# The last two heads of a linear attention: a sixteenth product per block, or spare rows of the attention output filled by way of DRAM

## The chip, the cores and the metric

The kernel runs on one core of a Trainium2 chip. Its time is what the device needs for one execution, in microseconds (us); the median of three runs before the change is 650.78 us, the lowest 650.26 and the highest 651.06. A core has TensorE (PE in the profile; PEld are its weight loads), VectorE (DVE), ScalarE (ACT), GpSimd (POOL) and SyncE (SP), which here only issues DMAs. "DMA" are the sixteen transfer engines that they share.

## The reference

The input `x` is 1 x 2048 x 640, layer-normalised, and goes into two branches. One is a linear attention of 32 heads of 20 with a feature map of two softmaxes; the other is a gelu MLP with 1536 hidden units. The result is `x + attention * silu(MLP)`.

```
q, k, v = (xn @ wqkv) split into 32 heads of 20
phi_q = concat[softmax(q w_phi), softmax(-q w_phi)]      (40 features a head; phi_k alike)
num = phi_q @ (phi_k^T v);  den = phi_q . sum_s phi_k + 1e-6
s = (num / den, heads side by side: 640 columns) @ wo
out = x + s * silu(gelu(xn @ w1 + b1) @ w2 + b2)
```

## The kernel before, in words

Most of the program (up to about 535 us of the profiled execution's span) makes queries, keys and values and runs eleven of the twelve units of the MLP. This study is about what comes behind: the twelfth unit's second matrix, the numerators of the attention, and the output projection. There the 2048 tokens are worked on in four chunks of 512, in `ORDER = (2, 3, 0, 1)`, and everything lies transposed: rows are features, columns are tokens.

The normalised query features lie in DRAM in one tensor per chunk, `phi_t[c]`, with 1280 rows (32 heads x 40). The four token tiles of each chunk write it (L1069, `phi_t<-eq`, from `q_norm`), and `load_phi` (L1086) reads it back: five loads of 240 rows (`phT<-phi_t`, 480 KB each, L1091, groups j = 0 to 4, three heads for each of two halves) and one of the last two heads' 80 rows (160 KB, L1093, j = 5).

`num` (L1097) makes the numerators. For j = 0 to 4 two products with the block-diagonal state `bdk` fill rows 0 to 63 and 64 to 127 of a PSUM bank. A half holds three heads, so 60 rows of it carry data and four are zero. ACT copies the bank to `oT` in the rounded form (L1106), and DVE writes what the rounding left as a second plane (L1107). Group j = 5, the last two heads, takes two products with `bdl` (L1110) and one more pair of evictions (L1112, L1113), into `oTl`, which holds its 40 rows three times in different roundings.

`finish` (L1145) makes a block of 128 output rows: for each j three products with `wo_s[j]` (high by high, high by low, low by high: `PASSES`), and a sixteenth, `wol` by `oTl`, which covers the three passes of the last two heads at once. Behind it DVE multiplies by the gate, POOL adds the residual (L1158, L1159), and SP stores the block. Five blocks (d = 0 to 4) make a chunk, and the numerators of the next chunk stand behind block 3 of each chunk.

Two more things matter. `make_wol` (L1077) makes `wol` from a loaded `raw` (L1074) with two DVE operations, a cast (`wolh`) and one that writes `wol`; before, both stand in the MLP's last `down` (L990). `down` works in the order d = 0 to 2 together, then 3, then 4, and its `mid` steps put other work between its products; the first chunk's `num` is one.

The order is written by hand: the program runs under a manual schedule, so that each engine does its instructions in the order in which the code issues them. All loads and stores of this part are issued by SP, in one order. SP's DMAs count on eight semaphores in turn, and each waits until the one eight places ahead of it has landed; a DMA that waits for an engine's result holds up every DMA behind it.

Of the kernel before, what the change touches and what calls it, by code (L numbers as in the profile page):

```python
# [15 lines left out]
P = 128  # L16
NT = S // P
NCH = 4
# [28 lines left out]
def hedgehog_gated_mlp_kernel(ctx: ExitStack, tc: tile.TileContext, x, xt_in, wqk, bd, wv, wo, w1, b1, w2, b2, out_t):  # L47
# [33 lines left out]
    def slab(dt, name, shape=(P, 2, D)):  # L81
        return slabs.tile(list(shape), dt, tag="S", name=name)
# [18 lines left out]
    wq_dram = dram.tile([2, P, 2, HALF], F32, name="wq_dram")  # L101
    z_dram = dram.tile([1440], F32, name="z_dram")
    st_dram = dram.tile([NT // 2, 2, P, 2], F32, name="st_dram")

    nc.gpsimd.memset(hmask, 1.0)
    nc.gpsimd.affine_select(out=hmask, in_=hmask, pattern=[[-DH, 6]], compare_op=OP.is_ge, fill=0.0, base=0,
# [872 lines left out]
    def act_lo(ps, hs):  # L979
        nc.vector.tensor_tensor(hs[:, 1], ps, hs[:, 0].bitcast(F32), op=OP.subtract)  # L980
        return hs
# [89 lines left out]
    def wol_raw():  # L1071
        raw = row([P, D], F32, "raw")
        for r in range(3):
            nc.sync.dma_start(raw[40 * r:40 * r + 40, :], wo[640:680, :])  # L1074
        return raw

    def make_wol(raw):  # L1077
# [4 lines left out]
                                       op0=OP.mult, op1=OP.add)  # L1082
        return wol


    def load_phi(c, js, home=None):  # L1086
        out = {}
        for j in js:
            ph = slab(F32, "phT", (P, 2, CW)) if home is None else home.tile([P, 2, CW], F32, tag="L", name="phT")
            if j < 5:  # L1090
                nc.sync.dma_start(ph[:120], phi_t[c][240 * j:240 * j + 240, :].rearrange("(e p) t -> p e t", p=120))  # L1091
            else:
                nc.sync.dma_start(ph[:80, 0], phi_t[c][1200:, :])  # L1093
            out[j] = ph
        return out

    def num(phi, oT, js):  # L1097
        for j in js:
            ph = phi.pop(j)
            po = bankB()  # L1100
            if j < 5:
                for e in range(2):
                    nc.tensor.matmul(po[64 * e:64 * e + 64, :], bdk[:120, 2 * j + e, :], ph[:120, e, :],  # L1103
                                     start=True, stop=True)
                o2 = oT[0][j]
                nc.scalar.activation(o2[:, 0], po[:], AF.Copy)  # L1106
                nc.vector.tensor_tensor(o2[:, 1], po[:], o2[:, 0].bitcast(F32), op=OP.subtract)  # L1107
            else:
                for a, b in ((0, 64), (64, 120)):
                    nc.tensor.matmul(po[a:b, :], bdl[:80, a:b], ph[:80, 0], start=True, stop=True)  # L1110
                o2 = oT[1]
                nc.scalar.activation(o2[:120, 0], po[:120], AF.Copy)  # L1112
                nc.vector.scalar_tensor_tensor(o2[:120, 1], o2[:120, 0].bitcast(F32), lowsel[:120, :],  # L1113
                                               po[:120], op0=OP.mult, op1=OP.add)

    JA, JB = (0, 1, 2), (3, 4, 5)

    def new_oT(home):
        return ([home.tile([P, 2, 512], F32R, tag="S" if home is slabs else "L", name="oT") for _ in range(5)],
                slab(F32R, "oTl", (P, 2, 512)))  # L1120

    xres, gates, wols = {}, {}, []
    ORDER = (2, 3, 0, 1)

    def load_res(i):
# [10 lines left out]
    def gate(i):  # L1136
        if i < NCH * KC:
            c, d = divmod(i, KC)
            c = ORDER[c]
            if c < 2:  # L1140
                y = ys[d][:, c, :]
                nc.scalar.activation(y, y, AF.Silu, bias=b2t[:, d:d + 1])
                gates[c, d] = y

    def finish(c, d, oT, last):  # L1145
        steps = [(wo_s[j][:, b, d * P:(d + 1) * P], oT[0][j][:, a, :]) for j in range(5) for a, b in PASSES]
        steps.append((wols[0][:120, d * P:(d + 1) * P], oT[1][:120, 1, :]))
        xr, gt = xres.pop((c, d)), gates.pop((c, d))
        end = last and d == KC - 1
        parts = (slice(0, W2), slice(W2, 512))  # L1150
        for k, sl in enumerate(parts):
            if end or k == 0:
                mv = sl if end else slice(0, 512)
                ps = bankB()
                for n, (w, o) in enumerate(steps):
                    nc.tensor.matmul(ps[:, mv], w, o[:, mv], start=n == 0, stop=n == 15, skip_group_check=True)  # L1156
            g = gt[:, sl]
            nc.vector.tensor_tensor(g, ps[:, sl], g, op=OP.mult)  # L1158
            (nc.vector if last else nc.gpsimd).tensor_tensor(xr[:, sl], g, xr[:, sl], op=OP.add)  # L1159
            if last:  # L1160
                nc.sync.dma_start(out_t[d * P:(d + 1) * P, c * CW + sl.start:c * CW + sl.stop], xr[:, sl])
        if not last:
            nc.sync.dma_start(out_t[d * P:(d + 1) * P, c * CW:(c + 1) * CW], xr[:])
# [20 lines left out]
    for unit in range(units):  # L1184
# [71 lines left out]
        if not more:  # L1256
            xstack.close()
            ctx.enter_context(tc.tile_pool(name="pad", bufs=1)).tile([P, 16], F32, name="lpad")
            late = ctx.enter_context(tc.tile_pool(name="late", bufs=13, reuse_waits="tile"))
# [4 lines left out]
        if not more:  # L1264
            wolr = wol_raw()
        turn(qdone)
        qdone = qs
        for t in QN.get(unit + 1, ()):
            qe[t] = q_load(t)
        next(w1f, None)  # L1270
        dn = down(g, w2g, hs, 0)
        next(dn)
        h12 = act_lo(*h12)
        next(q1, None)
        next(w1f, None)
# [47 lines left out]
    phin.update(load_phi(ORDER[1], JB))  # L1323
    gate(0)
    gate(1)

# [14 lines left out]

    lq = late_q((7,))
    for ci, c in enumerate(ORDER):
        if ci + 1 < NCH:
            oTn = new_oT(late if ci % 2 else slabs)
        for d in range(KC):
            load_res(ci * KC + d + 4)
            finish(c, d, oT, ci == NCH - 1 and d >= 3)
            next(lq, None)
            gate(ci * KC + d + 2)  # L1350
            if ci == 0 and d < 2:
                next(lq, None)
            if ci + 2 < NCH and d == 1:
                phi = load_phi(ORDER[ci + 2], JA, late if ci % 2 else None)
            if ci + 1 < NCH and d == 3:
                num(phin, oTn, range(6))
            if ci + 2 < NCH and d == 3:
                phin = {**phi, **load_phi(ORDER[ci + 2], JB)}
        if ci + 1 < NCH:
            oT = oTn  # L1360
    ffn.close()
# [2 lines left out]
def _layout(A_x, A_wqkv, A_w_phi, A_wo, B_w1, B_b1, B_w2, B_b2):  # L1364
    import numpy as np
    a = {k: np.asarray(v) for k, v in dict(x=A_x, wqkv=A_wqkv, wphi=A_w_phi, wo=A_wo, w1=B_w1, b1=B_b1,
                                           w2=B_w2, b2=B_b2).items()}
    wqk = np.zeros((2, KC, P, FOLD_W), a["wqkv"].dtype)
    bd = np.zeros((P, 6, DH), a["wphi"].dtype)
    wo = np.zeros((680, D), a["wo"].dtype)  # L1370
    for k in range(10):
        wo[64 * k:64 * k + 60] = a["wo"][60 * k:60 * k + 60]
    wo[640:] = a["wo"][600:]
# [38 lines left out]
```

## Time and profile before

| what | value |
|---|---|
| time, median of 3 runs (lowest, highest) | 650.78 us (650.26, 651.06) |
| span of the profiled execution, first to last instruction | 649.0 us |
| PE busy | 643.7 us (99%) |
| DVE, ACT, POOL busy | 485.1, 238.1, 408.9 us |
| DMA, mean of the span | 210 GB/s |

The profiled execution's own time is not listed apart from its span; the median of the runs lies 1.78 us above the span, and that difference is the work around the first and the last instruction. In the profile's timelines a row gives a start, a length, the engine, the line and the tiles, and the number of instructions; brackets give the idle time ahead of it on that engine and what ended it. Rows whose engine ends in q (SPq) are instructions of the engine's queue, such as the issue of a DMA. A full-precision product (L1103, L1110) appears as two matrix passes, so `x20` there are ten products.

### The profile page before, as it was taken

Reading aid. Unit: us, or ns where it says so; the run is one execution under the profiler, and the core shown is the slowest. Engines: PE = TensorE matmul, PEld = TensorE weight load, DVE = VectorE, ACT = ScalarE, POOL = GpSimd, SP = SyncE. Lnnn points to the kernel's source line nnn. Section 1 sums busy time; section 2 is a strip of 40 time slices with the busy share of each in tenths; the row PEclk is TensorE's granted clock in tenths of the full one; section 3 lists DMA queues with packets and bytes.
Section 4 is the critical chain, followed back from the end, with each engine's and each line's share of the span. In section 5 each row is a group of like instructions: output and inputs, shape, how many; then the busy total and the mean of one; then the engine's idle time right before and its main releaser. Section 6 shows DMA issues by size and latency. Waiting matters only on the chain.

```text
span 649.0 us, 11412 instructions
## 1 busy us (share of the span) xinstructions
PE 643.7 (99%) x4379; PEld 559.1 (86%) x4379; DVE 485.1 (75%) x736; ACT 238.1 (37%) x345; POOL 408.9 (63%) x375
## 2 busy tenths in 40 slices
PE   9999999999999999999999999999999999999997
PEld 9999999999999998888888888888888886766866
DVE  5887976789867787587988877768889899853132
ACT  3622423425243447244243346641231524032130
POOL 2876477897987756857878865355463966342321
PEclk9999999999999999999999999999999999999999
DMA  9477286494312477365986998794969499999952
GB/s 346 113 238 228 57 303 197 107 309 147 123 42 74 152 263 262 103 217 170 317 236 236 254 409 285 144 350 163 183 238 243 67 267 198 304 242 248 291 207 81
DMA packets 167119, 136.53 MB, mean 210 GB/s; under 512 B 89890, under 2 KB 131106, under 8 KB 166682
## 3 DMA queue, kind: packets, MB, share of 16 engines
q1 hardware_dynamic: 164330, 124.22, 65.9%
q10 hardware_dynamic: 2736, 11.60, 4.8%
q8 instruction: 34, 0.56, 0.4%
q14 instruction: 19, 0.16, 0.1%
HBM read 87.41 MB, written 48.38 MB: 209 GB/s over the span
## 4 chain that ended last, share of the span: by engine, by line
PE 96%; DMA 1%; DVE 1%; SPq 0%; issue 0%; DVEq 0%
PE pB L998 24%; PE pA L411 23%; PE pB L969 23%; PE pB L1156 11%; PE pA L724 6%; PE pB L1103 2%; PE pA L174 2%; PE kv L491 2%; PE qV L724 1%; DMA folds<-in_wqk_dram 1%; PE qY L724 1%; DVE y L1007 1%; PE pB L1110 1%; DMA phi_t<-eq 0%; PE pA L397 0%; DVE wolh L1080 0%
## 5 line engine op out<-in xcount | busy, mean ns | idle before, releaser
L998 PE MATMUL pB<-hs,w2s 128*128 128x512 f32 x720 | 165.7, 389 | 0.0
L998 PEld LDWEIGHTS pB<-hs,w2s 128*128 128x128 f32 x720 | 135.0, 188 | 28.8 <-DVE y L1007 0.8
L969 PE MATMUL pB<-xp,w1s 128*128 128x512 f32 x324 | 81.3, 389 | 0.0
L969 PE MATMUL pB<-xd,w1s 128*128 128x512 f32 x324 | 79.3, 389 | 0.0
L452 POOL TENSOR_TENSOR eq<-eq,rc 128x1280 f32<-128x1280 f32 x16 | 37.9, 2368 | 55.3 <-DVE rc L1060 38.1
L1156 PE MATMUL pB<-oT,wo 128*128 128x512 f32 (+1 forms) x315 | 72.3, 381 | 0.0
L969 PEld LDWEIGHTS pB<-xd,w1s 128*128 128x128 f32 x324 | 60.8, 188 | 12.6
L969 PEld LDWEIGHTS pB<-xp,w1s 128*128 128x128 f32 x324 | 60.8, 188 | 12.6
L1156 PEld LDWEIGHTS pB<-oT,wo 128*128 128x128 f32 x315 | 57.2, 188 | 13.8 <-PE pB L1103 2.5
L1007 DVE TENSOR_TENSOR y<-pB,y 128x512 f32<-128x512 f32 x100 | 63.1, 676 | 1.4 <-PE pB L998 1.4
L974 ACT ACTIVATE pB<-pB,b1t 128x512 f32<-128x512 f32 x48 | 31.8, 662 | 78.8 <-DVE pB L1237 28.9
L411 PE MATMUL pA<-wk,xp 128*128 128x320 f32 x384 | 59.6, 310 | 0.0
L439 ACT ACTIVATE e<-e 128x1280 f32<-128x1280 f32 x32 | 40.6, 1272 | 50.0 <-POOL e L430 50.0
L411 PEld LDWEIGHTS pA<-wk,xp 128*128 128x128 f32 x384 | 56.9, 188 | 0.1
L430 POOL TENSOR_TENSOR e<-nr,e 128x640 f32<-128x640 f32 x32 | 46.0, 1437 | 16.4 <-DVE nr L429 16.3
L452 POOL TENSOR_TENSOR e<-e,rc 128x1280 f32<-128x1280 f32 x16 | 37.8, 2369 | 20.2 <-DVE rc L479 20.2
L1047 POOL TENSOR_TENSOR ez<-eq,zrep 128x1280 f32<-128x1280 f32 x16 | 47.3, 2959 | 2.0 <-DMA eq<-e_dram 2.0
L519 POOL TENSOR_TENSOR w1s<-raw,w1s 128x640 fp32r<-128x640 f32 (+1 forms) x18 | 26.2, 1458 | 27.6 <-ACT w1s L518 27.6
L411 PE MATMUL pA<-wv,xp 128*128 128x320 f32 x240 | 37.0, 310 | 0.0
L1159 POOL TENSOR_TENSOR xres<-gt,xres 128x256 f32<-128x256 f32 x20 | 14.3, 735 | 35.3 <-DVE gt L1158 24.9
L149 POOL TENSOR_TENSOR w2s<-raw,w2s 128x640 fp32r<-128x640 f32 x23 | 36.1, 1592 | 0.2 <-ACT w2s L147 0.2
L411 PEld LDWEIGHTS pA<-wv,xp 128*128 128x128 f32 x240 | 35.5, 188 | 0.1
(190 smaller groups left out, 1140.4 us busy)
## 6 DMA issues: line engine op xcount, KB each, us to landing
raw<-in_w_dram SPq DMA_DIRECT2D x42, 320.0 KB, 6.7
e_dram<-e ACTq DMA_DIRECT2D x16, 640.0 KB, 3.9
eq<-e_dram SPq DMA_DIRECT2D x16, 640.0 KB
phi_t<-eq SPq DMA_DIRECT2D x64, 160.0 KB, 4.3
phT<-phi_t SPq DMA_DIRECT2D x20, 480.0 KB, 10.1
xt<-in_x_dram SPq DMA_DIRECT2D x16, 320.0 KB, 6.1
xres<-in_xt_dram SPq DMA_DIRECT2D x20, 256.0 KB, 9.1
out_dram<-xres SPq DMA_DIRECT2D x18, 256.0 KB, 5.1
```

The lines of the kernel that those rows point to most:

```text
L149: eng.tensor_tensor(sl[:, 1, :], raw, sl[:, 0, :].bitcast(F32), op=OP.subtract)
L411: nc.tensor.matmul(ps[:, hf, :HALF], stat_x(q, o, k, a), ws[k][:, b, hf * HALF:(hf + 1) * HALF], start=n == 0, stop=n == 3 * KC - 1)
L430: rest = lambda: nc.gpsimd.tensor_tensor(e5[:, :, :, 1, :], nr[:, :, :, None].to_broadcast([P, 2, 16, DH]), e5[:, :, :, 0, :], op=OP.subtract)
L439: nc.scalar.activation(ef, ef, AF.Exp)
L452: nc.gpsimd.tensor_tensor(e3, e3, rc[:, :, None].to_broadcast([P, 64, DH]), op=OP.mult)
L724: nc.tensor.matmul(bank[ch], q_x(blk, a, q), p_weight(base, f, w, k)[:, b], start=ch not in seen and n == 0, stop=n == len(mms) - 1, skip_ ...
L969: nc.tensor.matmul(bank[ch][:], tl[:, a, off + wo_:off + wo_ + P], mov(blk, b), start=new and n == 0, stop=n == len(mms) - 1, skip_group_c ...
L974: nc.scalar.activation(ps, ps, AF.Gelu_apprx_tanh, bias=b1t[:, f:f + 1])
L998: nc.tensor.matmul(ps[:], ws[i][:, b, d * P:(d + 1) * P], hs[o][i][:, a, :], start=i == n == 0, stop=(i, n) == (GF - 1, 2), skip_group_che ...
L1007: nc.vector.tensor_tensor(y, ps[:], y, op=OP.add)
L1047: nc.gpsimd.tensor_tensor(zv, ef, zf, op=OP.mult)
L1156: nc.tensor.matmul(ps[:, mv], w, o[:, mv], start=n == 0, stop=n == 15, skip_group_check=True)
```

## The change

Three of the four chunks (2, 3 and 0) lose the sixteenth product. Their last two heads' 40 rows go into the four spare rows of each half of `oT` (rows 60 to 63 and 124 to 127, five groups: 2 x 4 x 5 = 40 rows), and the host lays the matching rows of `wo` at those places. Chunk 1, the last one, keeps the product.

The 40 rows change partition on the way, and go through DRAM: `load_rest` loads the last two heads' features (`phR`) early, `num_rest` makes the rows (chunks 2 and 3 together in one bank, chunk 0 in another), evicts both planes to `oR` and stores them in `r_dram` (512 KB and 256 KB), and `put_rest` brings them into `oT` with two DMAs per chunk, each of four rows of 20 KB (`4x5120`). As rows 60 to 63 of a half are now written by a DMA, the evictions of these chunks go in two parts of 60 rows each. `oT` is one tile for all five groups, with two buffers. `make_wol` and its loads move behind the middle of the tail, the first `num` moves one step ahead in `down`, and `num` comes ahead of the gate in the loop.

```diff
+    def load_rest(*cs):
+        ph = slab(F32, "phR", (P, 2, CW))
+        for e, c in enumerate(cs):
+            nc.sync.dma_start(ph[:80, e], phi_t[c][1200:, :])
+        return ph, len(cs)
+    def num_rest(ph, n):
+        po, o2 = bankB(), slab(F32R, "oR", (P, 2, CW))
+        at = slice(0, 64 * n)
+        for e in range(n):
+            nc.tensor.matmul(po[64 * e:64 * e + 64, :], bdl[:80, :64], ph[:80, e, :], start=True, stop=True)
+        split_o(po, o2, at)
+        rest = r_dram[next(rests)]
+        nc.sync.dma_start(rest[at], o2[at].bitcast(F32).rearrange("p s t -> p (s t)"))
+        return rest
+    def split_o(po, o2, *parts):
+        for at in parts:
+            nc.scalar.activation(o2[at, 0], po[at], AF.Copy)
+        for at in parts:
+            nc.vector.tensor_tensor(o2[at, 1], po[at], o2[at, 0].bitcast(F32), op=OP.subtract)
+    def num(phi, oT, parts=(slice(0, 60), slice(64, 124))):
+        for j in range(KC):
...
+            split_o(po, oT[:, j], *parts)
+    def put_rest(oT, oR, r):
+        for e in range(2):
+            nc.sync.dma_start(oT[64 * e + 60:64 * e + 64].bitcast(F32).rearrange("p j s t -> p j (s t)"),
+                              oR[r + 20 * e:r + 20 * e + 20].rearrange("(i j) t -> i j t", j=KC))
-        steps.append((wols[0][:120, d * P:(d + 1) * P], oT[1][:120, 1, :]))
+        if c == ORDER[-1]:
+            steps.append((wol[:120, d * P:(d + 1) * P], oTl[:120, 1, :]))
...
-            phi = load_phi(ORDER[0], range(6))
+            phi = load_phi(ORDER[0], range(KC))
+            phr = load_rest(*ORDER[:2]), load_rest(ORDER[2])
...
         next(dn)
+        if not more:
+            rest.append(num_rest(*phr[0]))
...
         if not more:
+            rest.append(num_rest(*phr[1]))
             break
...
-    oT = new_oT(late)
-    phin = load_phi(ORDER[1], JA, late)
+    oT, oTn = oTs
+    put_rest(oT, rest[0], 0)
+    phin = load_phi(ORDER[1], JA)
...
     def first_num():
-        wols.append(make_wol(wolr))
-        yield
         yield
         yield
-        num(phi, oT, range(6))
+        num(phi, oT)
         yield
...
+            if ci == 1 and d == 4:
+                wolr = wol_raw()
+            if ci == 2 and d == 2:
+                wol = make_wol(wolr)
```

Where the instructions stand now is told by their order on each engine. On PE, from the last `down` on (`hs` by `w2s`) to the first blocks of the projection, before:

```order
L998 MATMUL pB<-hs,w2s 128x512 x48
L1103 MATMUL pB<-phT,bdk 64x512 x10
L1110 MATMUL pB<-phT,bdl 64x512
L1110 MATMUL pB<-phT,bdl 56x512
L998 MATMUL pB<-hs,w2s 128x512 x12
L1156 MATMUL pB<-oT,wo 128x512 x15
L1156 MATMUL pB<-oTl,wol 128x512
```

and the same place after the change, up to the second chunk's blocks:

```order
L999 MATMUL pB<-hs,w2s 128x512 x18
L1103 MATMUL pB<-phR,bdl 64x512 x2
L999 MATMUL pB<-hs,w2s 128x512 x12
L1103 MATMUL pB<-phR,bdl 64x512
L999 MATMUL pB<-hs,w2s 128x512 x6
L1129 MATMUL pB<-phT,bdk 64x512 x10
L999 MATMUL pB<-hs,w2s 128x512 x24
L1178 MATMUL pB<-oT,wo 128x512 x60
L1129 MATMUL pB<-phT,bdk 64x512 x10
```

The numerators of the first chunk now have 36 products of `down` ahead of them and 24 behind, where it was 48 and 12, and three products for the last two heads stand between the products of `down`.

On DVE, in the last unit, the first `y` of the row is that of d = 0. Before, from the last `hs` to the first chunk's evictions:

```order
L980 TENSOR_TENSOR hs_5782<-pB_5743,hs_5782 128x512 [waits DMAHW4_49,DMAHW6_49,DMAHW3_49,Activation_49]
L447 TENSOR_REDUCE dn_5844<-ez_5668 128x64 [waits Pool_49]
...
L1007 TENSOR_TENSOR y4_4732<-pB_5862,y4_4732 128x512 [waits PE_49]
L1080 CAST wolh_5903<-raw_5809 120x640 [waits DMAHW2_49,DMAHW3_49,DMAHW1_49,Pool_49]
L1081 SCALAR_TENSOR_TENSOR wol_5904<-wolh_5903,midsel_120,raw_5809 120x640 [waits DVE_49,Pool_49]
L1007 TENSOR_TENSOR y0_4683<-pB_5900,y0_4683 128x512 [waits PE_49]
```

and after:

```order
L1122 TENSOR_TENSOR oR_5847<-pB_5846,oR_5847 128x512 [waits DMAHW1_49,DMAHW4_49,DMAHW0_49,Activation_49]
L981 TENSOR_TENSOR hs_5787<-pB_5748,hs_5787 128x512 [waits DMAHW6_49]
L448 TENSOR_REDUCE dn_5854<-ez_5670 128x64 [waits Pool_49]
...
L1008 TENSOR_TENSOR y4_4734<-pB_5872,y4_4734 128x512 [waits PE_49]
L1122 TENSOR_TENSOR oR_5881<-pB_5880,oR_5881 64x512 [waits Activation_49]
L1122 TENSOR_TENSOR oT_5822<-pB_5921,oT_5822 60x512 [waits PE_49,Activation_49]
```

An eviction of `oR` that waits for ACT now stands ahead of the chain that ends in `y3` and `y4`; the two `wol` operations are gone from there, and ten half evictions of `oT` follow where five whole ones were.

On SP, from the stores of the last query tile of the first group to the loads of the second chunk's features, before:

```order
L1069 DMA phi_t_83<-eq 32x40x32 x8
L1091 DMA phT<-phi_t_85 120x2x512 x3
L1041 DMA eq<-e_dram 128x1280
L1130 DMA xres<-in_xt_dram 128x512
```

and after:

```order
L1070 DMA phi_t_83<-eq 32x40x32 x8
L1106 DMA r_dram_95<-oR 128x1024
L1106 DMA r_dram_96<-oR 64x1024
L1135 DMA oT<-r_dram_95 4x5120 x2
L1090 DMA phT<-phi_t_85 120x2x512 x3
L1042 DMA eq<-e_dram 128x1280
L1151 DMA xres<-in_xt_dram 128x512
```

Both stores of `oR` and the first two reads of them stand ahead of the second chunk's feature loads, and those wait in the same queue.

More of the change, by code (lines that the diff above doesn't have):

```diff
@@ L103, in hedgehog_gated_mlp_kernel @@
     st_dram = dram.tile([NT // 2, 2, P, 2], F32, name="st_dram")
+    r_dram = [dram.tile([P, 2 * CW], F32, name=f"r_dram{i}") for i in range(2)]
     nc.gpsimd.memset(hmask, 1.0)
@@ L1083, in make_wol, with load_phi @@
         return wol
-    def load_phi(c, js, home=None):
+    def load_phi(c, js):
         out = {}
         for j in js:
[L1089 to L1094, printed above, removed]
-        return out
@@ L1097, in num @@
-    def num(phi, oT, js):
-        for j in js:
+            out[j] = slab(F32, "phT", (P, 2, CW))
+            nc.sync.dma_start(out[j][:120], phi_t[c][240 * j:240 * j + 240, :].rearrange("(e p) t -> p e t", p=120))
+        return out
+    def load_rest(*cs):
[12 more added lines that the diff above has]
+        return rest
@@ new lines, in num_last @@
+    def num_last(ph):
+        po, o2 = bankB(), slab(F32R, "oTl", (P, 2, CW))
+        for a, b in ((0, 64), (64, 120)):
+            nc.tensor.matmul(po[a:b, :], bdl[:80, a:b], ph[:80, 0], start=True, stop=True)
+        nc.scalar.activation(o2[:120, 0], po[:120], AF.Copy)
+        nc.vector.scalar_tensor_tensor(o2[:120, 1], o2[:120, 0].bitcast(F32), lowsel[:120, :], po[:120],
+                                       op0=OP.mult, op1=OP.add)
+        return o2
+    def split_o(po, o2, *parts):
[3 more added lines that the diff above has]
+            nc.vector.tensor_tensor(o2[at, 1], po[at], o2[at, 0].bitcast(F32), op=OP.subtract)
@@ L1116, in hedgehog_gated_mlp_kernel @@
[L1116 to L1122, printed above, removed]
+            for e in range(2):
+                nc.tensor.matmul(po[64 * e:64 * e + 64, :], bdk[:120, 2 * j + e, :], ph[:120, e, :],
+                                 start=True, stop=True)
+            split_o(po, oT[:, j], *parts)
+    def put_rest(oT, oR, r):
+        for e in range(2):
+            nc.sync.dma_start(oT[64 * e + 60:64 * e + 64].bitcast(F32).rearrange("p j s t -> p j (s t)"),
+                              oR[r + 20 * e:r + 20 * e + 20].rearrange("(i j) t -> i j t", j=KC))
@@ L1123, in hedgehog_gated_mlp_kernel, with new_oT @@
+    JA, JB = (0, 1, 2), (3, 4)
+    def new_oT():
+        return late.tile([P, KC, 2, CW], F32R, tag="O", name="oT", bufs=2)
+    xres, gates, rests = {}, {}, iter(range(2))
     ORDER = (2, 3, 0, 1)
@@ L1270, in hedgehog_gated_mlp_kernel @@
         next(w1f, None)
+        if not more:
+            oTs = [new_oT(), new_oT()]
+            rest = []
         dn = down(g, w2g, hs, 0)
         next(dn)
+        if not more:
+            rest.append(num_rest(*phr[0]))
         h12 = act_lo(*h12)
@@ L1343, in hedgehog_gated_mlp_kernel @@
     for ci, c in enumerate(ORDER):
-        if ci + 1 < NCH:
-            oTn = new_oT(late if ci % 2 else slabs)
+        if 0 < ci < NCH - 1:
+            oTn = new_oT()
+            if ci == 1:
+                put_rest(oTn, rest[1], 0)
         for d in range(KC):
```

42 lines of the change are left out of this document (17 added, 25 removed).

## The prediction

> **What bounds the kernel now.** I began with the page's slices and its chain, then read the tail on PE's timeline, and then asked the chain, DVE, ACT and SP for the same stretch.
>
> ```profile
> PE   9999999999999999999999999999999999999997
> DMA  9477286494312477365986998794969499999952
> PE 96%; DMA 1%; DVE 1%; SPq 0%; issue 0%; DVEq 0%
> ```
>
> PE is full in every slice but the last and makes 96% of the chain that ended last. Work taken from PE is therefore time, unless PE then has to wait. The second row warns: a slice is 16 us, and from the 33rd (519 us) to the 38th the DMA engines are at 9 tenths or more too; only the last two slices are lower.
>
> ```profile
> 535.45 11.04 PE L998 MATMUL pB<-hs,w2s 128*128 128x512 f32 x48
> 546.42 4.51 PE L1103 MATMUL pB<-phT,bdk 120*64 120x512 f32 x20
> 551.32 1.07 PE L1110 MATMUL pB<-phT,bdl 80*64 80x512 f32 x4 [0.39 <-DVE y L1007]
> 555.18 3.56 PE L1156 MATMUL pB<-oT,wo 128*128 128x512 f32 x15
> ...
> 558.82 3.58 PE L1156 MATMUL pB<-oT,wo 128*128 128x512 f32 x15
> 562.24 0.40 PE L1156 MATMUL pB<-oTl,wol 120*128 120x512 f32 x1
> 562.47 3.58 PE L1156 MATMUL pB<-oT,wo 128*128 128x512 f32 x15
> ...
> 574.21 1.03 PE L1110 MATMUL pB<-phT,bdl 80*64 80x512 f32 x4
> 575.17 3.70 PE L1156 MATMUL pB<-oT,wo 128*128 128x512 f32 x15
> ...
> 617.41 4.51 PE L1103 MATMUL pB<-phT,bdk 120*64 120x512 f32 x20
> 621.75 1.03 PE L1110 MATMUL pB<-phT,bdl 80*64 80x512 f32 x4
> ```
>
> From these rows come PE's prices. A block of 16 lasts from 558.82 to 562.47, 3.65 us, so a product takes 0.228. The ten products of a chunk's numerators take 621.75 - 617.41 = 4.34 us, 0.434 each; the last two heads' pair 575.17 - 574.21 = 0.96, 0.48 each. PE waits in the tail once, 0.39 us, and not for a DMA.
>
> The chain of the last stretch shows who nearly bounds PE ahead of the projection:
>
> ```profile
> 542.38 1.19 DVE y L1007 x2
> ...
> 548.00 1.67 DVE wolh L1080
> ...
> 550.67 0.61 DVE y L1007
> ...
> 551.32 1.07 PE pB L1110 x2
> 552.40 2.95 PE pB L998 x12
> ```
>
> It runs along DVE until 551.28 and only then goes over to PE: DVE has no room there. Once DVE is let go, the next that could be late are the loads:
>
> ```profile
> 547.00:556.00 9.00, 8.61 (x40) 4.29 (x37) 8.88 (x13) 3.59 (x6) 2.31 (x1) 1.00 0.97 228
> 579.00:603.00 24.00, 24.00 (x107) 16.77 (x106) 7.92 (x17) 6.65 (x11) 7.15 (x10) 1.00 1.01 264
> 603.00:627.00 24.00, 24.00 (x107) 16.77 (x106) 8.27 (x17) 6.03 (x10) 7.13 (x10) 1.00 0.92 274
> ```
>
> The columns are length, busy PE, PEld, DVE, ACT, POOL, the granted clock (full), the DMA share and GB/s. The DMA engines work at 0.97, 1.01 and 0.92 of their time here, at 264 to 274 GB/s. What is added to them comes later by its own length.
>
> **The change, part by part.** *Products.* Three chunks of five blocks lose one product each: 15 x 0.228 = -3.43 us. The pairs of the second and third chunk leave PE's path: 2 x 0.96 = -1.92. That of the last chunk stays. The first region needs its own account.
>
> *The first region.* The rows are DVE's and ACT's:
>
> ```profile
> 540.31 0.67 DVE L980 TENSOR_TENSOR hs<-pB,hs 128x512 fp32r<-128x512 f32 x1
> ...
> 546.73 1.27 DVE L1007 TENSOR_TENSOR y<-pB,y 128x512 f32<-128x512 f32 x2
> 547.93 1.74 DVE L1080 CAST wolh<-raw 120x640 fp32r<-120x640 f32 x1
> 549.78 0.88 DVE L1081 SCALAR_TENSOR_TENSOR wol<-wolh,midsel,raw 120x640 fp32r<-120x640 f32 x1
> ...
> 552.38 3.07 DVE L1107 TENSOR_TENSOR oT<-pB,oT 128x512 fp32r<-128x512 f32 x5
> 538.23 3.24 ACT L147 ACTIVATE wo<-raw 128x640 fp32r<-128x640 f32 x5
> 547.55 0.60 ACT L1106 ACTIVATE oT<-pB 128x512 fp32r<-128x512 f32 x1 [6.08 <-PE pB L1103]
> ```
>
> PE reaches the numerators at 535.45 + 36 x 0.228 + 3 x 0.48 = 545.1, and their fourth group, six products on, at 547.7. That group's bank is the one that DVE frees with the `y` of d = 3. DVE now has the eviction of `oR` ahead of it, which needs ACT's copy, and ACT is at its five splits of `wo` until 541.47 and copies until 542.07. DVE ends `oR` (0.6 as a whole eviction: 3.07 over five) at 542.7 and starts `hs` there, not at 540.31. From `hs` to the end of that `y` it needs 546.73 + 0.64 - 540.31 = 7.06, so the bank is free at 549.74 and PE stands for 2.0 us. Behind it come two groups (1.74) and 24 products (5.48): the first block starts at 556.96, against 555.18, **+1.8** net, with the old 0.39 gone in it. If the early features land late by up to 1 us, that hides under the same wait. Without the wait on ACT the region would give -0.2; with DVE 1 us later than this, +2.8.
>
> *Half evictions.* Ten of 0.61 are 6.1 us for 3.07. In a transition they start one group behind the numerators' start, and the fifth group is ready about 8 us after it; PE needs it after ten products, one block of 15 and twelve products, 4.34 + 3.42 + 2.74 = 10.5 us. Hidden. Were that cover gone, 2 to 3 us a transition.
>
> *SP and the DMA.* The costly part, I think, is the order on SP.
>
> ```profile
> 538.48 8.30 SPq L1069 DMA_DIRECT2D phi_t<-eq  x8
> 546.88 1.82 SPq L1091 DMA_DIRECT2D phT<-phi_t  x3
> ...
> 609.23 0.32 SPq L1093 DMA_DIRECT2D phT<-phi_t  x1
> ...
> 618.20 0.33 SPq L1130 DMA_DIRECT2D xres<-in_xt_dram  x1
> 618.71 0.34 SPq L1163 DMA_DIRECT2D out_dram<-xres  x1
> ```
>
> Now both stores of `oR` stand between the first two rows, and the second waits for DVE's second `oR`, two evictions (the `y` of d = 4 and itself) behind the bank's release: 549.74 + 2 x 0.61 = 551.0. With that store, two reads and their issue (about 0.45 each), the second chunk's feature loads leave SP at about 552.5, 5.6 us later, and so does all that follows. Extra bytes behind that: the 256 KB store, 1.0 us at 270 GB/s; six reads of 80 KB. No transfer of four rows is in the trace. Spread over all sixteen engines 80 KB take 0.3 us; if each row goes through one engine, its 20 KB take 1.2 us at a sixteenth of 270 GB/s, and the rest follows. I take 0.5, near the spread end, 3.0 for six. The second and third chunk's 160 KB loads are now early: -1.2. Together 8.4 us.
>
> Some of this is won back: while SP stands, the queue runs empty and the loads behind it start at once (the first three landed 5.1 us after issue before, half of it queue), and the share of 0.92 leaves 1.9 us of 24. I take 3.4 back, and keep 5.0 of lateness at the last chunk's loads. How much slack had they? An SP issue waits for the eighth DMA ahead of it; the row at 618.71 is the eighth behind the one at 609.23, which is the last load of the last chunk, and the row ahead of it is let go by the load before:
>
> ```profile
> SPq L1130 <- DMA phT<-phi_t: 5.6, 4, 2.3
> ```
>
> So these two landed by about 618.2 and 618.7, and PE needed them at 617.41 + 8 x 0.434 = 620.9 and 621.75: a slack of 2.8 us, the smallest of the tail. And PE now comes 1.8 - 14 x 0.228 - 1.92 = 3.3 us earlier. PE's waits for features, at the third and fourth chunk's numerators together: 5.0 - 2.8 + 3.3 = **+5.5**. The ends of this term: 0, if all is won back, and 9 to 10, if nothing is.
>
> By a rule of the Trainium skill, page "DMA: Bandwidth & Descriptors", section "Why a DMA increments its semaphore by 16 and not by 1", a transfer uses as many engines as the largest number up to 16 that divides the outer size of both its sides. By it these reads of four rows run on four engines, the 1.2 us end, and the sum would be 4.2 us more. The trace of before can't show it, having no such transfer.
>
> *`wol` moved.* Its loads now stand behind the last features, and on DVE the cast and its partner (1.74 + 0.88) stand ahead of the last chunk's evictions. If the 300 KB (1.1 us at 270 GB/s) land 1.2 us after the last group's load, the first eviction is ready 1.2 + 2.62 + 0.76 + 0.61 = 5.2 us after that load, and PE wants it after two group products, the pair and a block, 0.87 + 0.96 + 3.42 = 5.25: free. If a store and a load are ahead of them, and they land 2.7 us after, PE waits **1.5**. I take that; the ends are 0 and 2.4 (3.6 us after).
>
> *Sum.* -3.43 - 1.92 + 1.8 + 5.5 + 1.5 = +3.4. On the profiled execution that is 649.0 + 3.4 = 652.4 of span; what lies around the span (1.78) stays, so 650.78 + 3.4 = **654.2 us**.
>
> **The rivals.** *The loads keep up.* Then the last two terms go: 650.78 - 3.43 - 1.92 + 1.8 = 647.2 us. For it: before, SP often waited for POOL and DVE and not for the DMA, and such waits can swallow a shift. Against it: the shares of 0.97 to 1.01.
>
> *Nor does ACT hold DVE.* A further -2.0: 645.2 us. The split of `wo` would have to end 2 us earlier than its row; nothing moves it.
>
> *One engine per row.* Six reads at 1.2 in place of 0.5 add 4.2: 658.4 us. It decides if the engines that carry the rows are as full as the others, which the shares say. Its sign would be a delay of every load behind such a read.
>
> *Half of the lateness is won back.* The term of 5.5 falls to about 2.5 and `wol` costs 1: 650.7 us, no change.
>
> *The change doesn't do what it says* only if the loads' order kept PE's products, and PE's order shows 15 a block.
>
> **How the numbers follow.** Chances: the forecast 0.48 (its own range 652.2 to 657), one engine per row 0.12, half won back 0.10, loads keep up 0.25, neither wait 0.05. A measurement of this kernel tells about 0.2% (1.3 us) from no change. Faster by more than that: 0.30; within: 0.10; slower: 0.60. The range goes from 646.9, so that the second rival lies outside and the first just inside, to 659.5, which holds the rule's 658.4 and a little of the unhidden 9 to 10.
>
> **What would show it.** On PE's timeline the first block should start near 557, behind a wait for DVE `y` of about 2 us ahead of the fourth numerator group. SP's waits should show L1106 waiting for DVE `oR` for some 4 to 5 us until about 551. PE's waits should name DMA `phT` at the third or fourth chunk's numerators (2 to 9 us together), and DVE's the `raw` ahead of `wolh`. Blocks should last 3.42. The forecast is wrong if PE never waits for a DMA behind 560 us; then the time is near 647. If every load behind a four-row read lands late by a microsecond or more, the rival of one engine per row holds.

## The result, and the profile after

The change makes the kernel slower: 667.0 us (median of 4 runs, 665.79 to 667.89) against 650.87 before; the ratio is 1.0247, 95% interval 1.0232 to 1.0261. The forecast was 654.2 with a range to 659.5. The direction was forecast, the size was not: +16.1 us in place of +3.4. Medians below are over the fast executions: run 8 and run 14 each had one slow one (2428.38 and 718.51 us).

The page of the changed kernel first, with its chain:

```profile
span 665.9 us, 11408 instructions
PE 82%; DMA 12%; SPq 2%; DVE 1%; POOL 1%; issue 0%; ACT 0%; POOLq 0%; ACTq 0%
```

PE made 96% of the chain before and makes 82% now; 12% are DMAs. Three rows tell what PE waits for in the tail (line waited at, releaser, us in total, times, longest):

```profile
PE pB L1129 <- DMA phT<-phi_t: 6.8, 5, 2.9
PE pB L1178 <- ACT y L1163: 2.3, 1, 2.3
PE pB L1103 <- DMA phR<-phi_t: 2.0, 2, 1.2
```

Before there was one wait of 0.39 us, for DVE. The places are on PE's timeline:

```profile
540.80 1.07 PE L1103 MATMUL pB<-phR,bdl 80*64 80x512 f32 x2 [1.17 <-DMA phR<-phi_t]
542.66 1.80 PE L1103 MATMUL pB<-phR,bdl 80*64 80x512 f32 x2 [0.78 <-DMA phR<-phi_t]
...
560.95 13.87 PE L1178 MATMUL pB<-oT,wo 128*128 128x512 f32 x60
574.75 3.65 PE L1129 MATMUL pB<-phT,bdk 120*64 120x512 f32 x16
580.74 1.98 PE L1129 MATMUL pB<-phT,bdk 120*64 120x512 f32 x4 [2.34 <-DMA phT<-phi_t]
582.64 17.82 PE L1178 MATMUL pB<-oT,wo 128*128 128x512 f32 x75
...
612.64 13.88 PE L1178 MATMUL pB<-oT,wo 128*128 128x512 f32 x60 [2.29 <-ACT y L1163]
626.45 2.79 PE L1129 MATMUL pB<-phT,bdk 120*64 120x512 f32 x12
632.10 1.98 PE L1129 MATMUL pB<-phT,bdk 120*64 120x512 f32 x4 [2.85 <-DMA phT<-phi_t]
...
637.98 8.92 PE L1178 MATMUL pB<-oT,wo 128*128 128x512 f32 x30
```

The products are as cheap as forecast (60 from 560.95 to 574.75, 0.230 each). But in this execution the first block starts at 560.95, 5.8 us later than before (run 3 comes back to this), and every one of the three numerator stages behind it stands for its features: from 574.75, 600.40 and 626.45 they need 7.9, 6.2 and 11.5 us (the last with the pair), where ten products need 4.3.

What holds the loads is seen on SP, where the eighth DMA behind another cannot be issued before that one has landed:

```profile
547.82 4.51 SPq L1106 DMA_DIRECT2D r_dram<-oR  x2
552.44 1.16 SPq L1135 DMA_DIRECT2D oT<-r_dram  x2
553.69 1.31 SPq L1090 DMA_DIRECT2D phT<-phi_t  x3
555.10 0.38 SPq L1042 DMA_DIRECT2D eq<-e_dram  x1
555.53 0.42 SPq L1151 DMA_DIRECT2D xres<-in_xt_dram  x1
556.00 0.42 SPq L1155 DMA_DIRECT2D gt<-g_dram  x1
558.20 0.33 SPq L1151 DMA_DIRECT2D xres<-in_xt_dram  x1
560.88 0.32 SPq L1155 DMA_DIRECT2D gt<-g_dram  x1
562.69 0.33 SPq L1151 DMA_DIRECT2D xres<-in_xt_dram  x1
565.05 0.32 SPq L1155 DMA_DIRECT2D gt<-g_dram  x1
```

The row at 558.20 is the eighth behind the first read of four rows, the one at 560.88 behind the second; the next two stand for feature loads of 480 KB. So the second read's 80 KB landed 2.7 us behind the first, a longer step than those of the 480 KB loads behind it (1.8 and 2.4).

The trace also has the moments at which the parts of a DMA are complete. Each of the two reads has four such events, each load 15. Of the first load's fifteen, eleven come from 559.38 to 559.94 and the other four only from 561.34 to 562.67; the two loads behind it show the same split into eleven and four. Before the change all fifteen of each of these three loads came within 0.9 us. Taking one event for one engine, the reads hold up four of the engines that the loads need, and a load is there only when its last part is.

### The profile page after: what moved, and what is told of

Its sections match the earlier page's. It is cut to its first block, busy times and chain, and to the rows that moved or that the text cites. A ratio compares the mean times of both kernels' runs of the same rounds, so it can differ in the third digit from the quotient of the medians.

```text
span 665.9 us, 11408 instructions
## 1 busy us (share of the span) xinstructions
PE 650.0 (98%) x4358; PEld 558.9 (84%) x4358; DVE 492.5 (74%) x750; ACT 246.1 (37%) x359; POOL 408.3 (61%) x375
## 4 chain that ended last, share of the span: by engine, by line
PE 82%; DMA 12%; SPq 2%; DVE 1%; POOL 1%; issue 0%; ACT 0%; POOLq 0%; ACTq 0%
PE pA L412 23%; PE pB L999 21%; PE pB L970 20%; PE pA L725 6%; DMA phT<-phi_t 4%; PE pB L1178 4%; DMA gt<-g_dram 3%; PE pA L175 2%; DMA phR<-phi_t 2%; SPq L1070 2%; PE kv L492 2%; DMA out_dram<-xres 1%; PE qV L725 1%; DMA raw<-in_wo_dram 1%; PE qY L725 1%; PE pB L1129 1%
## 5 line engine op out<-in xcount | busy, mean ns | idle before, releaser
L1178 PEld LDWEIGHTS pB<-oT,wo 128*128 128x128 f32 x315 | 58.8, 194 | 18.6 <-issue 4.4
L1120 ACT ACTIVATE oT<-pB 60x512 fp32r<-60x512 f32 (+1 forms) x35 | 20.7, 592 | 61.8 <-issue 32.8
```

## The experiments

Each edit is to the changed kernel unless it says otherwise; the kernel before, measured beside these runs, took 650.3 to 650.8 us. Theory A: the reads of four rows are the loss. Theory B: the store on which SP stands is. Theory C: the first region is late because of the last two heads' loads.

**1. No reads.** The kernel leaves out the last two heads of three chunks; whole evictions put zeros into the spare rows.

```diff
-    def num(phi, oT, parts=(slice(0, 60), slice(64, 124))):
+    def num(phi, oT, parts=(slice(0, P),)):
...
     def put_rest(oT, oR, r):
+        pass
```

> The changed kernel without the six reads into the spare rows; the evictions write all 128 rows, so that the spare rows hold zeros and the last two heads are left out of three chunks. Theory A (each read of four rows keeps four DMA engines for some 2.5 to 3 us, and every load behind it lands later by that): the PE waits at the second to fourth chunk's numerators go, 12 to 13 us of them with the clock that falls after a wait, so 654 to 655 us. Theory B (the store that waits for DVE stands in SP's queue, and the reads cost little): only 1 to 3 us go, 664 to 666 us.

Measured 648.6 us, ratio 0.9979 (0.9962 to 0.9995). All of the loss goes, and more than A expected; the store that waits is still in its place, so B alone cannot be it. Not all of it need be the reads': the two profiled spans differ by 19.4 us, and 3.8 of these lie ahead of the first read, since here the first block starts at 557.12 (run 3). PE's waits of this kernel, and the same 7 us in this kernel and (last row) in the changed one (length, busy PE, PEld, DVE, ACT, POOL, clock, DMA share, GB/s):

```profile
PE pB L1129 <- DMA phT<-phi_t: 0.7, 1, 0.7
PE pB L1103 <- DMA phR<-phi_t: 0.5, 1, 0.5
```

```profile
553.00:560.00 7.00, 7.00 (x32) 5.79 (x31) 3.46 (x5) 0.00 (x0) 0.00 (x0) 1.00 1.03 265
```

```profile
553.00:560.00 7.00, 7.00 (x33) 4.49 (x30) 6.62 (x10) 4.90 (x9) 0.00 (x0) 1.00 0.90 155
```

With the reads the DMA engines move 155 GB/s there, without them 265. Run 1 is 3.7 us ahead at that point; in the 7 us that lie as far behind its own loads' issue (549.3 to 556.3) it moves 220 GB/s at a share of 0.90, so the share does not tell the two apart. In 7 us some 0.5 MB less is moved.

**2. Reads of one row, cut small, on SP.** The scratch tensor is `[P, 4, 272]`, with 256 of 272 used, so that a row of `oT` comes in 20 pieces.

```diff
+            for i in range(4):
+                p, q = 64 * e + 60 + i, r + 20 * e + 5 * i
+                nc.sync.dma_start(oT[p:p + 1] ... "p (n u) -> p n u", u=256,
+                                  oR[q:q + 5, :, :256] ... "(a j) c u -> a (j c) u", a=1)
```

> The same bytes, each chunk's two reads of four rows cut into eight reads of one row in 20 pieces of 1 KB (the scratch tensor has a gap behind every 1 KB for it). Theory A: ten engines share each row, a read takes 0.1 to 0.3 us, and the time falls to 655 to 658 us. Theory B: nothing is won, and the 18 more issues on SP cost 0 to 3 us, 667 to 670 us.

Measured 668.87, ratio 1.0291 (1.0268 to 1.0314). A's number is missed. But SP's row says what took the place:

```profile
550.81 5.99 SPq L1137 DMA_DIRECT2D oT<-r_dram  x8
556.90 1.41 SPq L1090 DMA_DIRECT2D phT<-phi_t  x3
```

Eight issues take 6 us, and the feature loads leave at 556.9, later still than in the changed kernel (553.7). Behind these reads the loads themselves are not held: they land as soon after their issue as without reads, and their fifteen events come together (the table in run 10). For the first chunk, then, A's mechanism is gone as expected, and SP's time for the issues has taken its place.

**3. The last two heads' loads first.**

```diff
-            phi = load_phi(ORDER[0], range(KC))
             phr = load_rest(*ORDER[:2]), load_rest(ORDER[2])
+            phi = load_phi(ORDER[0], range(KC))
```

> The three loads of the last two heads' features go ahead of the first chunk's five feature loads on SP. Theory C (the first region's 4 us beyond my sum are PE and DVE waiting for these loads): the first block starts at 556.5 to 558 in place of 560.9. If nothing behind it bounds, the time falls by 3 to 4 us to 663 to 664; by theory A the loads behind the reads are still late and most of it comes back as waits for phT, 665 to 667 us.

Measured 664.55, ratio 1.0211 (1.0195 to 1.0227). PE's waits for `phR` are gone, and the numerators are through at 550.1, against 555.3 in the changed kernel. But C is not shown by that. Run 1 has these loads in the old order, and up to its first read the changed kernel differs from it in the evictions alone; here are the rows behind the numerators in the changed kernel, in run 1 and in this run:

```profile
555.28 5.74 PE L999 MATMUL pB<-hs,w2s 128*128 128x512 f32 x24
551.50 5.78 PE L999 MATMUL pB<-hs,w2s 128*128 128x512 f32 x24
550.12 5.78 PE L999 MATMUL pB<-hs,w2s 128*128 128x512 f32 x24
```

In runs 2, 4, 5, 6, 10 and 12, with the old order too, this row starts between 550.6 and 551.4. So the 555.3 is the one profiled execution of the changed kernel, in which `phR` landed late; why it did stays open. Against the others the new order gains 0.5 to 1.4 us there. The time falls by 2.4 us; PE now waits for the reads and then for `phT` (8.0 us in all):

```profile
558.05 15.47 PE L1178 MATMUL pB<-oT,wo 128*128 128x512 f32 x60 [2.16 <-DMA oT<-r_dram]
```

**4. The store late.** The store of the second `oR` moves behind the four residual loads.

```diff
+    rest[1] = rest[1]()      # the store, behind load_res
```

> The store of the second oR goes behind the second chunk's first loads and the residual loads, so that SP does not stand for DVE's second oR ahead of them. Theory B: SP issues the second chunk's loads some 3 to 4 us earlier, and the time falls by 3 to 5 us to 662 to 664. Theory A: the two reads of four rows still stand ahead of them; 0 to 2 us, 665 to 667 us.

Measured 662.32, ratio 1.0179 (1.0162 to 1.0196). B's number is met: with the reads there, the time falls by 4.7 us (3.0 against run 10, which keeps the store in its place and has the early first region, as this run has). Without the reads it costs little: runs 5 and 11 differ by 2.2 us, with the edit of run 3 in it. It is lateness on a queue that the reads have already made late.

**5. The half evictions alone.** As run 1 (the two heads left out), with `parts=(slice(0, 64), slice(64, P))`.

> As the run without reads, but with the evictions still in two parts, of 64 rows each, so that no spare row stays unwritten; the last two heads are again left out of three chunks. It prices the half evictions alone. Theory of the prediction (hidden by the block and the ten products): within 1 us of the run with whole evictions, 648 to 650 us. Rival (they, and not the reads, were what the run without reads took away): 655 us or more.

Measured 648.93, ratio 0.9976 (0.9965 to 0.9988), 0.3 us from run 1: hidden, as forecast.

**6. The reads from ACT's queue.**

```diff
-            nc.sync.dma_start(oT[64 * e + 60:64 * e + 64]
+            nc.scalar.dma_start(oT[64 * e + 60:64 * e + 64]
```

> The six reads of four rows unchanged, but issued by ACT instead of SP, so that they are in another queue than the loads. Theory A1 (the loads are late because they stand behind the reads in SP's queue on four engines): most of the loss goes, 650 to 655 us. Theory A2 (the four engines lack the throughput, whichever queue feeds them): 658 to 666 us.

Measured 665.3, ratio 1.021 (1.0179 to 1.0241). Near A2: another queue changes 1.7 us at most. Here too four of a load's fifteen parts come last (the second load: eleven by 557.33, four from 561.16 to 569.85).

**7.** With the edits of 3 and 4 besides:

> Reads of four rows from ACT, the last two heads' loads first, the second store late: the three edits together. By the gains of each alone (2.5 for the loads, 4.7 for the store, and what the queue gives): 646 to 652 us under A1, 654 to 660 under A2.

Measured 661.82, ratio 1.0172 (1.0157 to 1.0188); both numbers missed. A new wait takes the gain: ACT's DMAs count on the same eight semaphores as SP's, ACT stood 14 us for one that a residual load held, and PE with it.

```profile
561.67 5.46 PE L999 MATMUL pB<-hs,w2s 128*128 128x512 f32 x12 [8.58 <-DVE oT L1125]
568.30 13.86 PE L1181 MATMUL pB<-oT,wo 128*128 128x512 f32 x60 [1.18 <-DMA oT<-r_dram]
```

**8.** The same with the reads of run 2:

> The loads first, the store late, and the reads of one row in 20 pieces, issued by ACT. On SP such a read took 0.7 us to issue and landed 2.5 us later, so the DMA engines are hardly held, but ACT issues 24 of them, 5 to 6 us a chunk, and the evictions behind them wait. 646 to 650 us if ACT's time is spare; 653 to 660 if the evictions come late.

Measured 666.33, ratio 1.0242 (1.0225 to 1.0259). The wait at that place was 17.4 us; this run tells nothing of the reads.

**9. The first chunk's reads from SP, the others from ACT**, with 3 and 4:

> The loads first, the store late, the second chunk's and third chunk's reads from ACT and the first chunk's from SP, so that ACT no longer stands ahead of the first evictions (in the run with all reads on ACT it stood 14 us for a semaphore that a residual load held, and PE 8.6 us behind it). From the first block on, that run needed 86.7 us to PE's end; with the first block at 556 to 557 that gives PE's end at 643 to 645 and 649 to 651 us.

Measured 663.06, ratio 1.0205 (1.0166 to 1.0245). Missed: the first block starts at 557.6, near what was expected, but `phT` is late again (8.5 us of waits), though only two of the six reads stood in SP's queue. The queue is not what makes them dear.

**10. Reads of four rows in pieces of 1 KB, on SP.**

```diff
+            nc.sync.dma_start(oT[64 * e + 60:64 * e + 64] ... "p (n u) -> p n u", u=256,
+                              oR[r + 20 * e:r + 20 * e + 20, :, :256] ... "(i j) c u -> i (j c) u", j=KC)
```

> The changed kernel with the same two reads of four rows a chunk on SP, but each row cut into 20 pieces of 1 KB. If the cost is that four engines carry the bytes, the time stays within 2 us of the changed kernel, 665 to 669. If it is the size of the packets (20 KB each, during which an engine moves nothing else), a read takes about a quarter less or better and the time falls to 655 to 660.

Measured 665.31, ratio 1.0227 (1.0212 to 1.0242): the size of the packets is not it. The loads tell the same. For the second chunk's first three, from issue to the last completion event:

| kernel | reads ahead of the loads | us to landing | last parts of the first load |
|---|---|---|---|
| run 1 | none | 5.2, 6.8, 8.3 | all 15 within 0.6 us |
| changed | two of four rows | 9.0, 11.0, 12.4 | four of 15 come 1.4 to 2.7 us behind the rest |
| run 10 | two of four rows, 1 KB pieces | 8.8, 10.7, 12.2 | four of 15 come 1.3 to 2.3 us behind the rest |
| run 2 | eight of one row | 4.7, 6.3, 8.0 | all 15 within 0.5 us |

A pair of reads of four rows costs these loads 3.8 to 4.2 us in the changed kernel, 2 us a read, and the pieces change little of it.

**11. The ceiling:** no reads (the two heads left out), half evictions, and the edits of 3 and 4.

> No reads (the last two heads left out of three chunks), half evictions of 64 rows, the loads first and the store late: what is left if the transfer cost nothing and the first region were mended. Products and pairs by their rows, 650.7 - 3.4 - 1.9 = 645.4, and the first region within 1 us of before: 645 to 647 us.

Measured 646.72, ratio 0.994 (0.9923 to 0.9956). This is what the idea could give if the transfer were free: 0.6%.

**12. One pair of reads**, the first chunk's; half evictions for all three. The kernel leaves out the last two heads of the second and third chunk.

```diff
-    put_rest(oTn, rest[0], 64)
...
-                put_rest(oTn, rest[1], 0)
+                pass
...
-                num(phin, oTn)
+                num(phin, oTn, (slice(0, 64), slice(64, P)))
```

> The changed kernel with the first chunk's two reads only; the second and third chunk's last two heads are left out, their evictions in halves of 64 rows. If the loss is the reads' (18 us for six), a third of the dose gives 653 to 657 us. If it is a threshold that the first pair alone passes, 660 or more; if the first pair is free, 648 to 650.

Measured 654.48, ratio 1.0065 (1.004 to 1.009): 5.6 us above run 5 for two reads, 18.1 for six. The loss goes with the dose. The wait of 2.29 us that the changed kernel's row puts down to ACT, at the third chunk's first block (612.64), is gone here, where that chunk has no reads. It was for them: the last part of these reads is complete at 612.39.

**13. The spread reads from GpSimd's queue**, with 3 and 4: the edit of run 2 with

```diff
-                nc.sync.dma_start(oT[p:p + 1]
+                nc.gpsimd.dma_start(oT[p:p + 1]
```

> The loads first, the store late, and the 24 reads of one row in 20 pieces issued by GpSimd's queue. On SP such reads landed 0.2 us apart when they stood queued; what they cost there was SP's 0.7 us for each issue, ahead of the feature loads. If the price of the four-row reads is that four engines carry them, and nothing else in the way through DRAM costs, this comes within 1 to 3 us of the run without reads in the same order (646.7): 647 to 650 us, and no PE wait for phT over 1 us. If bytes that end in one partition are slow on any number of engines, or the way through DRAM costs by itself, 654 to 660 us.

Measured 656.9, ratio 1.0101 (1.0084 to 1.0118): the best time of all kernels that move the rows for all three chunks. It lies 7 us above what was expected if the number of engines were the whole price, and inside the other range, 654 to 660: bytes that end in one row being slow on any number of engines, or a cost of the way through DRAM itself. PE never waits for `phT`, and waits once, for the first chunk's reads:

```profile
563.71 16.50 PE L1183 MATMUL pB<-oT,wo 128*128 128x512 f32 x60 [7.77 <-DMA oT<-r_dram]
580.14 4.51 PE L1132 MATMUL pB<-phT,bdk 120*64 120x512 f32 x20
```

**14.** The same from SP:

> The same, but the 24 reads issued by SP. If SP's issue time is the price, the first chunk's eight stand 5 to 6 us ahead of the second chunk's loads: 654 to 659 us. If issue is free, the same time as from GpSimd.

Measured 669.34, ratio 1.0281 (1.0249 to 1.0313), slower than expected; `phT` is waited for 8.6 us. SP's first eight issues take 6 us, and the loads behind them leave at 556.39, against 546.50 in run 13. Taking the 24 issues off SP is worth some 12 us.

**15. The first chunk by two reads of four rows from SP (in pieces), the others spread from GpSimd**, with 3 and 4:

> As the run with all 24 spread reads on GpSimd's queue, where PE waited once, 7.8 us for the first chunk's reads; here the first chunk's come as two reads of four rows from SP, ahead of the second chunk's loads, and only the other sixteen from GpSimd. If two four-row reads cost what they cost in the run with one pair (5.6 us, some of it met by the loads first and the late store): 649 to 652 us. If the spread reads from GpSimd also cost something unseen: 653 or more.

Measured 662.75, ratio 1.0181 (1.0167 to 1.0196). The lower range is missed, the other (653 or more) met: beside the reads from GpSimd, issued at 551.7, the first chunk's come late (PE waits 5.7 us), and then `phT` (6.4).

**16. Spare rows for the second and third chunk only**, the first chunk as before the change, with whole evictions, `num_last` and 16 products a block; spread reads from GpSimd:

```diff
-        if c == ORDER[-1]:
+        if c in (ORDER[0], ORDER[-1]):
...
-            phr = load_rest(*ORDER[:2]), load_rest(ORDER[2])
+            phr = load_rest(ORDER[0]), load_rest(*ORDER[1:3])
...
-        num(phi, oT)
+        num(phi, oT, (slice(0, P),))
+        wols.append(num_last(phr[0][0]))
```

> The spare rows for the second and third chunk only; the first and the last keep the sixteenth product, wol is made where it was before, one store of oR, and 16 spread reads from GpSimd. PE's work falls by ten products and one pair, 2.3 + 0.96 = 3.2 us; DVE has one eviction more in the first region, 0.6. If the engines' share was the cause and no transfer is late: 647.5 to 649, faster than before. If GpSimd's reads land late for the second chunk: 651 to 656.

Measured 660.23, ratio 1.0154 (1.013 to 1.0179). Missed, and this is the run that limits the theory: the first block starts at 555.69, 0.5 us later than before, and yet

```profile
PE pB L1129 <- DMA phT<-phi_t: 7.5, 4, 2.6
```

Issued from GpSimd, the spread reads still go with late loads. The lateness has another look here: the load issued at 588.39, beside the third chunk's reads, takes 11.0 us, where the one at that place took 8.5 before, and all its fifteen events come together, from 597.65 to 599.38, with no four of them behind. That PE's one stop of 7.8 us in run 13 let the loads catch up is argued, not shown. No version that moves the rows beat the kernel before.

## Why the prediction was right in direction and wrong in size

By its own steps:

- *Products and pairs, -3.43 and -1.92.* Right. The ceiling of run 11, 646.7, lies 1.3 us above the 645.4 that they give.
- *First region, +1.8.* In the profiled execution 560.95 - 555.18 = +5.8, and not by the step that the forecast had: there is no wait of PE for a `y`, in this or in any other run, at the fourth numerator group. What came late was `phR`. PE waited 1.17 and 0.78 us for it, its products then ran slower (12 of `down` in 3.91 us, 3.02 in run 3), and DVE stood 4.84 us, until 545.13, since PE could make the second half only when the second chunk's `phR` had come:

```profile
545.13 0.69 DVE L1122 TENSOR_TENSOR oR<-pB,oR 128x512 fp32r<-128x512 f32 x1 [4.84 <-ACT oR L1120]
```

  I had let a late `phR` hide under the wait for `y`. In the runs where `phR` was not so late (run 12: `oR` at 541.69, `y` of d = 3 done by 547.9, the fourth group wanted at 549.0), `y` was in time. Without reads the first block then starts 1.9 and 1.6 us later than before (557.12 in run 1, 556.82 in run 5). That the size agrees is luck: it arises on PE, from the wait for `phR` (0.46 in run 1) and from the three products of the last two heads (2.4 there, 1.44 in the forecast).
- *Half evictions hidden.* Right (run 5).
- *SP stands, loads 5.6 us later.* The issue moved from 546.88 to 553.69, 6.8, with the late `phR` in it; in run 12 it moved to 551.05, 4.2. Right in kind, with the measured sizes on either side.
- *"I take 0.5, near the spread end, 3.0 for six."* This is the first step that failed. Both ends of its range, 0.3 and 1.2, were too low: the first pair made the loads behind it 3.8 to 4.2 us late, some 2 a read, and six reads cost 14 to 18 us of time (18.4 by run 1, 3.8 less if the late first region is taken out), 5.6 a pair (run 12). I had divided the rate of all sixteen engines by sixteen, 1.2 us for 20 KB. A 20 KB packet took 1.9 us on average (24 in the trace, 0.88 to 2.98), and the two reads of a pair fall to the same engines: the second one's four packets start at 555.22, 555.41, 556.09 and 556.36, when the first one's four end. The trace's completion events say how many carry one: a read of four rows has four, the 120-row loads have 15, the 40-row loads of `raw` 10 and the 128-row loads 16.
- *By the rule of the Trainium skill* ("DMA: Bandwidth & Descriptors", "Why a DMA increments its semaphore by 16 and not by 1") the reads were to run on four engines. These counts agree. The rival that I made of it, one engine per row, had the mechanism, and its sign came: the three loads behind the first pair were late by more than a microsecond each. But its price of 1.2 a read, 2.4 a pair, was too low as well, and it got a chance of 0.12.
- *PE's waits for features, +5.5.* Measured 6.8, of which 2.3 at the second chunk, where I had none. The size is near by luck: PE came late itself, by the first region and by products that ran slower, and that hid part of the loads' lateness.
- *3.4 us are won back.* Not seen; the queue lost time where it was to win it (155 GB/s behind the reads). The premise was misread too: of the three loads before only the first landed 5.1 us after its issue, the others took 6.3 and 7.8.
- *`wol`, 1.5.* Wrong. DVE waited 13.7 us for `raw`, but the first evictions of the last chunk were ready before PE came, late itself.
- *What was left out.* This is the second step that failed, a term put at nothing: behind its waits PE is slower. From the first block to PE's end the changed kernel needs 101.0 us and run 1, without reads, 85.5. Of these 15.5 us 9.1 are named waits (6.8 and 2.3; run 1 has 0.7). The rest is in products that run slower: the same 386 of them keep PE busy for 91.9 us at a mean granted clock of 0.93, and for 84.8 at 1.00 in run 1. These 7.2 us are more than half of what the forecast was short of. Where it happens:

```profile
578.00:583.00 5.00, 2.66 (x7) 0.68 (x6) 4.62 (x7) 2.90 (x6) 0.59 (x1) 0.74 0.54 119
626.00:638.00 12.00, 8.86 (x28) 2.08 (x26) 0.32 (x1) 2.98 (x5) 2.81 (x4) 0.73 1.02 308
638.00:650.00 12.00, 12.00 (x47) 9.79 (x46) 6.88 (x14) 3.66 (x6) 4.28 (x6) 0.84 0.50 177
```

  The clock column falls to 0.74, 0.73 and 0.84; 30 products at 637.98 take 8.92 us in place of 7.14 in run 1.

Shown: the reads are most of the loss, 14 to 18 us, by leaving them out and by dose; the first pair of four rows holds the loads behind it in four of their fifteen parts, whatever the size of the packets, and the first reads of one row from SP do not (run 10's table); another queue does not free them of it (run 6); half evictions are free (run 5). Argued, and in part against a run: that the share of engines is the whole price. The reads of one row have ten completion events when SP issues them, but sixteen from GpSimd, so there the events do not tell the engines; and in run 16 PE still waits 7.5 us for `phT`. What the reads from GpSimd hold, or whether it is the way into one row or through DRAM, stays open; and the second and third pair's share of the loss is known from run 12's dose only.

## What to carry to other kernels

Where the DMA engines are full and the bound engine has 3 us of slack, count a transfer by the engines that carry it and by what is queued on those, not by its bytes: 480 KB in six reads of four rows cost 14 to 18 us to save 5. A wait of the bound engine can cost more than its length, since the clock can fall behind it (9.1 us of waits, 7.2 us of slower products here); put that into the sum. And before work goes to DRAM and back, run it once with the way back left out: that ceiling (0.6% here) tells what the transfer may cost.

## What the runs showed of the hardware

A DMA share near 1.0 doesn't tell how many bytes the engines move: 0.90 went with 155 GB/s in the changed kernel and with 220 at the same distance behind the issue in run 1. Cutting a transfer into 20 pieces a row made its issue dearer: 0.75 us each on SP (8 in 5.99), where the plain reads took 0.25 to 0.69. And the granted clock stayed low after a wait: in run 13 the wait of 7.8 us, until 563.71, is followed by

```profile
564.00:572.00 8.00, 8.00 (x25) 6.32 (x25) 1.99 (x3) 0.00 (x0) 2.13 (x5) 0.67 1.06 231
572.00:580.00 8.00, 8.00 (x37) 6.46 (x35) 5.03 (x8) 0.00 (x0) 5.67 (x5) 1.00 1.06 234
```

with 0.67 and then 1.00. In slices of 1 us it is 0.50 up to 569, 0.87 in the next and 1.00 from 570 on, so it was halved for some 5.5 us behind the wait. The 60 products there take 16.50 us in place of run 1's 13.76: 2.7 us on top of the wait. In the changed kernel the wait of 2.34 us that ends at 580.74 is followed by two slices at 0.50 (581 to 583), but the one of 2.29 that ends at 612.64 by none (1.00 from 612 to 620).
